# Output products of a SwiGLU feed-forward in three fp32r passes instead of one fp32 product, with the factors made on ScalarE and GpSimd

## The chip, the cores and the metric

The kernel runs on one core of one Trainium2 chip. The metric is the device time of one execution in microseconds (us). Times are medians. PE is TensorE, DVE is VectorE, ACT is ScalarE and POOL is GpSimd.

A ratio of two kernels is the mean time of one kernel's runs over the mean of the other's in the same rounds. So it is not quite the ratio of the medians that are quoted beside it.

## The reference

```python
B, N, m, C = 4, 12416, 32, 128              # x: (B, N, C), inducing: (m, C)
def mab(q, kv):
    s = scale * (q @ kv.transpose(0, 2, 1))
    a = softmax(s)                           # exp after the max is taken off, sum + 1e-9
    return a @ kv
h = mab(I, x); y = mab(x, h)                 # attention over 32 inducing points and back

# y is (B*N, 128) = 49664 tokens; feed-forward with d_ff = 1536, weights given as float64
xn = y / sqrt(mean(y * y) + 1e-6) * rms_g
out = (silu(xn @ w_gate) * (xn @ w_val)) @ w_out
```

## The kernel before

The tokens are cut into 100 units, 25 for each of the four batches: 80 of 512 tokens, 16 of 480 and 4 of 256. A unit goes through 12 blocks of 128 hidden features. One block is a pair of fp32r products (gate, value), a silu on ScalarE, a product on VectorE and one fp32 output product that accumulates over the 12 blocks.

```python
ps_gv = pool("ps_gv", 4, space=PSUM)    # four banks, shared by gate and value products
ps_acc = pool("ps_acc", 2, space=PSUM)
ps_m = pool("ps_m", 2, space=PSUM)      # attention products beside the feed-forward
# ...
for j in range(NJ):                     # NJ = 12 blocks of a unit
    g = ps_gv.tile([P, 512], F32, name="gv", tag="gv")
    nc.tensor.matmul(g[:, 0:T], sg[:, ts(j, P)], a[:, 0:T], start=True, stop=True)   # fp32r
    v = ps_gv.tile([P, 512], F32, name="gv", tag="gv")
    nc.tensor.matmul(v[:, 0:T], sv[:, ts(j, P)], a[:, 0:T], start=True, stop=True)   # fp32r
    sl = silp.tile([P, 512], F32, name="silu")
    nc.scalar.activation(sl[:, 0:T], g[:, 0:T], AF.Silu)
    t = up.tile([P, 512], F32, name="u")
    nc.vector.tensor_tensor(out=t[:, 0:T], in0=sl[:, 0:T], in1=v[:, 0:T], op=ALU.mult)
    for _ in range(slot(j)):            # output products of earlier blocks, 0 to 2 of them
        if late:
            late.pop(0)()
    late.append(lambda j=j, t=t: project(j, t))     # fp32: acc += wo[j]^T t
```

`slot` also places the attention of the next batch and the "seams" among the blocks. A seam is the softmax, the norm and the split of the next 2048 tokens; one comes every four units. Ahead of each big exp of the attention the kernel holds output products back, so that PE has work while ScalarE is busy with the exp and with loading tables. Instructions stay in the order in which the program makes them. Which PSUM bank a new tile gets is decided when the program is built; below, "the built order" is the order of the instructions and of the banks in that program. The "flow" is the feed-forward's main part, from about 100 us on.

## Time and profile before

| | before |
|---|---|
| median of 3 runs | 1749.03 us (1748.61 to 1749.57) |
| PE / ACT / DVE / POOL busy | 99 / 44 / 66 / 10% |
| mean granted PE clock | 0.997 |
| chain of work that ended last | 92% PE |

These are the three lines of the view of PE's waits that the change is going to touch (what waits, for what: us in all, times, longest us):

```profile
PE gv L530 <- ACT silu L534: 2.9, 4, 0.9
...
PE acc L514 <- DVE u L536: 1.6, 1, 1.6
PE gv L532 <- ACT silu L534: 1.4, 7, 0.2
```

L530 is the gate product, L532 the value product, L514 the output product. In 1747 us PE waits for a silu eleven times, 4.3 us in all.

### The profile page before, as it was taken

Reading aid. Unit: us, or ns where it says so; the run is one execution under the profiler, and the core shown is the slowest. Engines: PE = TensorE matmul, PEld = TensorE weight load, DVE = VectorE, ACT = ScalarE, POOL = GpSimd, SP = SyncE. Lnnn points to the kernel's source line nnn. Section 1 sums busy time; section 2 is a strip of 40 time slices with the busy share of each in tenths; the row PEclk is TensorE's granted clock in tenths of the full one; section 3 lists DMA queues with packets and bytes.
Section 4 is the critical chain, followed back from the end, with each engine's and each line's share of the span. In section 5 each row is a group of like instructions: output and inputs, shape, how many; then the busy total and the mean of one; then the engine's idle time right before and its main releaser. Section 6 shows DMA issues by size and latency. Waiting matters only on the chain.

```text
span 1747.0 us, 20705 instructions
## 1 busy us (share of the span) xinstructions
PE 1722.2 (99%) x6454; PEld 973.6 (56%) x6454; DVE 1145.6 (66%) x1985; ACT 765.6 (44%) x1281; POOL 175.6 (10%) x134
## 2 busy tenths in 40 slices
PE   9899999999999999999999999999999999999998
PEld 7545555555565555555556555555556555555555
DVE  4857765666667776666666776566756666656655
ACT  4344445334544445443454444533354444444444
POOL 0311110102101101001010010110201101100100
PEclk9899999999999999999999999999999999999999
DMA  6334462133343145214334316322211121121111
GB/s 243 85 67 79 92 130 54 43 79 66 65 78 62 37 88 119 37 40 99 60 62 81 57 28 130 79 47 63 52 31 33 28 43 30 30 38 36 25 35 23
DMA packets 389340, 112.47 MB, mean 64 GB/s; under 512 B 365136, under 2 KB 369776, under 8 KB 386672
## 3 DMA queue, kind: packets, MB, share of 16 engines
q1 hardware_dynamic: 388944, 111.02, 31.6%
q8 instruction: 51, 0.84, 0.2%
q14 instruction: 57, 0.47, 0.1%
q10 hardware_dynamic: 288, 0.15, 0.0%
HBM read 53.95 MB, written 27.00 MB: 46 GB/s over the span
## 4 chain that ended last, share of the span: by engine, by line
PE 92%; ACT 3%; DVE 2%; DMA 1%; issue 1%; POOL 0%; ACTq 0%; DVEq 0%; POOLq 0%
PE acc L514 55%; PE gv L530 15%; PE gv L532 15%; PE mm L284 2%; PE mm L459 1%; PE mm L341 1%; DMA xn<-in_x_dram 1%; ACT silu L534 1%; PE acc L163 1%; DVE u L536 1%; ACT sc L313 1%; ACT L534 0%; ACT sc L394 0%; PE gv L341 0%; PE mm L407 0%
## 5 line engine op out<-in xcount | busy, mean ns | idle before, releaser
L514 PE MATMUL acc<-u,wo 128*128 128x512 f32 (+2 forms) x2400 | 1199.5, 583 | 3.9 <-POOL wo L241 2.1
L536 DVE TENSOR_TENSOR u<-silu,gv 128x512 f32<-128x512 f32 (+2 forms) x1200 | 798.6, 670 | 559.0 <-ACT silu L534 553.0
L534 ACT ACTIVATE silu<-gv 128x512 f32<-128x512 f32 (+2 forms) x1200 | 699.8, 585 | 931.2 <-DVE u L536 534.8
L530 PE MATMUL gv<-a,sg 128*128 128x512 f32 (+2 forms) x1200 | 919.8, 767 | 5.2 <-ACT silu L534 2.9
L514 PEld LDWEIGHTS acc<-u,wo 128*128 128x128 f32 x2400 | 440.1, 188 | 159.7 <-issue 64.5
L532 PE MATMUL gv<-a,sv 128*128 128x512 f32 (+2 forms) x1200 | 467.2, 389 | 1.9 <-ACT silu L534 1.4
L530 PEld LDWEIGHTS gv<-a,sg 128*128 128x128 f32 x1200 | 227.0, 189 | 279.8 <-issue 261.8
L532 PEld LDWEIGHTS gv<-a,sv 128*128 128x128 f32 x1200 | 227.8, 190 | 276.0 <-issue 186.3
L465 POOL TENSOR_TENSOR z<-z,sc 128x512 f32<-128x512 f32 (+2 forms) x27 | 32.0, 1187 | 1052.3 <-DVE z L464 1012.3
L473 POOL TENSOR_TENSOR rs<-ms,mhalf 128x16 f32<-128x16 f32 (+2 forms) x28 | 75.6, 2700 | 90.8 <-DVE ms L471 90.8
L517 DVE STREAM_TRANSPOSE o<-acc 128x512 f32<-128x512 f32 (+2 forms) x100 | 69.2, 692 | 1.1 <-PE acc L514 0.8
L387 POOL TENSOR_TENSOR sc<-sc,mx 128x512 f32<-128x512 f32 (+2 forms) x24 | 23.2, 968 | 315.8 <-DVE mx L386 244.2
L267 DVE STREAM_TRANSPOSE xT<-xT 128x512 f32<-128x512 f32 (+2 forms) x84 | 53.2, 633 | 0.0
L163 PE MATMUL acc<-ident 128*128 128x128 f32 x220 | 28.0, 287 | 1.4 <-POOL mhalf L150 1.4
L163 PEld LDWEIGHTS acc<-ident 128*128 128x128 f32 x220 | 26.9, 201 | 2.6 <-POOL mhalf L150 1.4
L459 PE MATMUL mm<-eT,gram 128*128 128x512 f32 (+2 forms) x56 | 26.8, 559 | 1.1 <-DVE eT L449 1.1
L284 PE MATMUL mm<-xT,hT 128*32 128x512 f32 (+2 forms) x192 | 26.8, 591 | 0.0
L477 POOL TENSOR_TENSOR sc<-sc,rs 128x512 f32<-128x512 f32 (+2 forms) x27 | 26.4, 976 | 2.1
L341 PE MATMUL mm<-xn,e 128*32 128x128 f32 x582 | 20.7, 276 | 0.0
L284 PE MATMUL mm<-xT,indT 128*32 128x512 f32 (+2 forms) x168 | 20.0, 547 | 0.0
L481 DVE STREAM_TRANSPOSE aT<-sc 128x512 f32<-128x512 f32 (+2 forms) x28 | 18.5, 660 | 1.3 <-POOL sc L477 1.3
L341 PEld LDWEIGHTS mm<-xn,e 128*32 128x32 f32 x582 | 15.0, 109 | 7.7 <-PE gv L530 5.5
(142 smaller groups left out, 432.5 us busy)
## 6 DMA issues: line engine op xcount, KB each, us to landing
out_dram<-o SPq DMA_DIRECT2D x320, 64.0 KB, 2.0
xT<-in_x_dram SPq DMA_DIRECT2D x60, 256.0 KB, 4.6
xn<-in_x_dram SPq DMA_DIRECT2D x60, 256.0 KB, 6.0
a<-hi SPq DMA_DIRECT2D x160, 64.0 KB, 2.0
a<-lo SPq DMA_DIRECT2D x158, 64.0 KB, 2.0
w<-w SPq DMA_DIRECT2D x22, 256.0 KB, 3.4
xn<-in_x_dram SPq DMA_DIRECT2D x5, 1024.0 KB, 11.1
out_dram<-o SPq DMA_DIRECT2D x64, 60.0 KB, 2.0
```

The lines of the kernel that those rows point to most:

```text
L163: nc.tensor.matmul(ps[:, 0:P], ident[:], ident[:], start=True, stop=True)
L267: nc.vector.transpose(out=t[:, ts(k, n * m)], in_=t[:, ts(k, n * m)])
L284: nc.tensor.matmul(ps[ts(q, m), 0:w], lhsT, xT[b, s][:, ts(q, w)], start=True, stop=True)
L341: nc.tensor.matmul(ps[ts(t % R, m), 0:C], e[:, ts(t, m)], xn[:, t, :], start=head and t < R, stop=not more)
L459: nc.tensor.matmul(ps[rows, 0:w], gram[b][rows, rows], st["eT"][rows, 0:w], start=True, stop=True)
L473: nc.gpsimd.tensor_tensor(out=rs, in0=ms, in1=mhalf[rows, 0:n], op=ALU.pow)
L514: nc.tensor.matmul(acc[:, 0:T], wo[:, j, :], t[:, 0:T], start=(j == 0), stop=(j == NJ - 1))
L517: nc.vector.transpose(out=o[:, 0:T], in_=acc[:, 0:T])
L530: nc.tensor.matmul(g[:, 0:T], sg[:, ts(j, P)], a[:, 0:T], start=True, stop=True)
L532: nc.tensor.matmul(v[:, 0:T], sv[:, ts(j, P)], a[:, 0:T], start=True, stop=True)
L534: nc.scalar.activation(sl[:, 0:T], g[:, 0:T], AF.Silu)
L536: nc.vector.tensor_tensor(out=t[:, 0:T], in0=sl[:, 0:T], in1=v[:, 0:T], op=ALU.mult)
```

## The change

The intent is to take work off PE, which is the bound. An fp32 product is four passes through the array, an fp32r product one (the prediction says where the four comes from; in the chain of the kernel before the two take 0.86 and 0.23 us). The change splits weight and input into a high part and a low part and forms the product with three fp32r passes instead of four, by Karatsuba's identity. With w = wh + wl/4096 and u = hi + lo:

w u = (1 + 1/4096) (wh hi + wl lo) + (wl - wh) (hi/4096 - lo)

The first two passes need a PSUM bank of their own. ScalarE takes that bank out at the end of the unit with the factor 1 + 1/4096, and VectorE adds the rest. The bank is taken from the attention, which is left with one. Up to four blocks of a unit are split (j = 0, 3, 6, 9), where a small model of GpSimd's time at build says that the factors will be ready.

```diff
+    KJ = range(0, NJ - 2, 3)
+    SLOT, SPLIT = 1.25, 2.9
-    ps_m = pool("ps_m", 2, space=PSUM)
+    ps_u = pool("ps_u", 1, space=PSUM)
+    ps_m = pool("ps_m", 1, space=PSUM)
 ...
+        def project3(j, hi, lo, d):
+            if st["k"] == nk:
+                st["u"] = ps_u.tile([P, 512], F32, name="u3")
+            ups, i, w = st["u"], KJ.index(j), kws["w"]
+            nc.tensor.matmul(ups[:, 0:T], w[:, i, :], hi, start=st["k"] == nk, stop=False)
+            st["k"] -= 1
+            nc.tensor.matmul(ups[:, 0:T], w[:, NK + i, :], lo, start=False, stop=not st["k"])
+            if not st["k"]:
+                o = st["o"] = outp.tile([P, 512], F32, name="o")
+                nc.scalar.activation(o[:, 0:T], ups[:, 0:T], AF.Copy, scale=1.0 + 2.0 ** -12)
+            project(w[:, 2 * NK + i, :], d)
 ...
         def project(lhsT, rhs):
 ...
+                if nk:
+                    nc.vector.tensor_tensor(out=o[:, 0:T], in0=acc[:, 0:T], in1=o[:, 0:T], op=ALU.add)
-                nc.vector.transpose(out=o[:, 0:T], in_=acc[:, 0:T])
+                nc.vector.transpose(out=o[:, 0:T], in_=(o if nk else acc)[:, 0:T])
 ...
+        def three(j, t):
+            nc.scalar.activation(hi, v, AF.Copy, scale=1.0 - 2.0 ** -13)
+            nc.gpsimd.tensor_tensor(out=lo, in0=v, in1=hi.bitcast(F32), op=ALU.subtract)
+            def rest():                 # one slot later
+                nc.scalar.activation(hs[:, 0:T], hi.bitcast(F32), AF.Copy, scale=2.0 ** -12)
+                nc.gpsimd.tensor_tensor(out=d, in0=hs[:, 0:T], in1=lo.bitcast(F32), op=ALU.subtract)
+                kara.append((ready[b, u, j], lambda: project3(j, hi, lo, d)))
 ...
-                if hold and len(late) < LAG or len(late) < 2:
-                    return 0
-                return 2 if len(late) > 2 else 1
+                count = max(len(plain) - 1, 0) + sum(at <= now for at, _ in kara)
+                if hold and count < LAG - 1:
+                    return
+                for _ in range(min(count, 2)):
+                    if kara and kara[0][0] <= now:
+                        kara.pop(0)[1]()
+                    else:
+                        plain.pop(0)()
```

Left out are the splitting of the weights, the build-time model, and the steps of the attention, which are moved by a few slots.

More of the change, by code (lines that the diff above doesn't have):

```diff
@@ L89 @@
     NU = len(units)
+    KJ = range(0, NJ - 2, 3)
+    NK = len(KJ)
+    SLOT, SPLIT = 1.25, 2.9
     def pool(name, bufs, **kw):
@@ L103 @@
     halves = pool("halves", 1)
-    astk = pool("astk", 3)
+    astk = pool("astk", 2)
+    third = pool("third", 1)
     silp = pool("silp", 3)
-    up = pool("up", LAG + 2)
+    up = pool("up", LAG + 3)
     outp = pool("outp", 2)
@@ L121, in load_rows @@
         n = per[s]
-        t = xnat[b, s] = xnp.tile([P, n, C], F32, name=f"xn{s}")
+        t = xnat[b, s] = xnp.tile([P, 16 if b and n > 4 else n, C], F32, name=f"xn{s % 2 if b and n > 4 else s}")
         if b or s == full:
             for q in range(R):
-                nc.sync.dma_start(out=t[ts(q, m), :, :], in_=of(xrows, b, s)[q])
+                nc.sync.dma_start(out=t[ts(q, m), 0:n, :], in_=of(xrows, b, s)[q])
         else:
@@ L247 @@
     flowing = []
+    lent = []
     def attention(b, load_next):
@@ L258, in bank @@
             if flowing:
+                assert not lent
                 return ps_m.tile([P, 512], F32, name="mm", tag="mm")
@@ L361, in turn_h, with scale_h, square_h @@
             nc.vector.tensor_copy(out=hT[:], in_=ps[:, 0:P])
-        def square_h():
+            if b:
+                scale_h()
+        def scale_h():
             hg = st["hg"] = once.tile([P, P], F32, name="hg")
             nc.vector.tensor_scalar_mul(out=hg[:], in0=st["ps"][:, 0:P], scalar1=gam[:])
+        def square_h():
+            if not b:
+                scale_h()
             gram[b] = small.tile([P, P], F32, name="gram")
@@ L457, in square @@
         def square():
+            assert not lent
+            lent.append(s)
             ps = st["ps"] = ps_m.tile([P, 512], F32, name="mm", tag="mm")
@@ L462, in turn_z @@
             ps = st["ps"]
+            lent.clear()
             z = st["z"] = work.tile([P, n, m], F32, name="z", tag="work")
@@ L496, in gather, with split_wo @@
             queue.dma_start(out=a[ts(k, m), 0:w].bitcast(F32), in_=half[ts(q, m), 0:w].bitcast(F32))
-    late, waiting = [], []
+    plain, kara, waiting = [], [], []
+    kws = {}
     def soon(k, step):
         waiting.append([k, step])
+    def split_wo():
+        w = kws["w"] = xnp.tile([P, 3 * NK, C], F32R, name=f"xn{full - 1}")
+        whi, wlo, ws = (w[:, ts(k, NK), :] for k in range(3))
+        wk = wo[:, KJ.start:KJ.stop:KJ.step, :]
+        nc.vector.tensor_scalar_mul(out=whi, in0=wk, scalar1=1.0 - 2.0 ** -13)
+        nc.vector.tensor_tensor(out=wlo, in0=wk, in1=whi.bitcast(F32), op=ALU.subtract)
+        nc.vector.tensor_scalar_mul(out=wlo, in0=wlo.bitcast(F32), scalar1=4096.0)
+        nc.vector.tensor_tensor(out=ws, in0=wlo.bitcast(F32), in1=whi.bitcast(F32), op=ALU.subtract)
+        for k, name in enumerate(("hi", "lo", "d")):
+            kws[name] = xnp.tile([P, 4, 512], F32R, name=f"xn{full - 4 + k}")
     def ffn(b, u, slot):
@@ L511, in ffn, with project @@
         acc = ps_acc.tile([P, 512], F32, name="acc")
-        def project(j, t):
-            nc.tensor.matmul(acc[:, 0:T], wo[:, j, :], t[:, 0:T], start=(j == 0), stop=(j == NJ - 1))
-            if j + 1 == NJ:
-                o = outp.tile([P, 512], F32, name="o")
-                nc.vector.transpose(out=o[:, 0:T], in_=acc[:, 0:T])
-                soon(2, lambda: store(o))
+        nk = sum((b, u, j) in ready for j in range(NJ))
+        st = {"left": NJ, "k": nk}
+        if nk:
+            st["o"] = None
+        def project(lhsT, rhs):
+            nc.tensor.matmul(acc[:, 0:T], lhsT, rhs, start=st["left"] == NJ, stop=st["left"] == 1)
+            st["left"] -= 1
+            if not st["left"]:
+                o = st["o"] if nk else outp.tile([P, 512], F32, name="o")
+                if nk:
+                    nc.vector.tensor_tensor(out=o[:, 0:T], in0=acc[:, 0:T], in1=o[:, 0:T], op=ALU.add)
+                nc.vector.transpose(out=o[:, 0:T], in_=(o if nk else acc)[:, 0:T])
+                soon(2, lambda: store(o))
+        def project3(j, hi, lo, d):
[9 more added lines that the diff above has]
+            project(w[:, 2 * NK + i, :], d)
         def store(o):
@@ L526, in store @@
                 nc.sync.dma_start(out=d[:, :, ts(k, m)], in_=o[ts(k, m), 0:T].rearrange("p (t c) -> p t c", c=m))
+        def three(j, t):
+            n = kws["n"] = (kws.get("n", 0) + 1) % 4
+            hi, lo, d = (kws[name][:, n, 0:T] for name in ("hi", "lo", "d"))
+            v = t[:, 0:T]
+            nc.scalar.activation(hi, v, AF.Copy, scale=1.0 - 2.0 ** -13)
+            nc.gpsimd.tensor_tensor(out=lo, in0=v, in1=hi.bitcast(F32), op=ALU.subtract)
+            def rest():
+                hs = third.tile([P, 512], F32, name="hs")
+                nc.scalar.activation(hs[:, 0:T], hi.bitcast(F32), AF.Copy, scale=2.0 ** -12)
+                nc.gpsimd.tensor_tensor(out=d, in0=hs[:, 0:T], in1=lo.bitcast(F32), op=ALU.subtract)
+                kara.append((ready[b, u, j], lambda: project3(j, hi, lo, d)))
+            soon(1, rest)
         for j in range(NJ):
@@ L536, in ffn @@
             nc.vector.tensor_tensor(out=t[:, 0:T], in0=sl[:, 0:T], in1=v[:, 0:T], op=ALU.mult)
-            for _ in range(slot(j)):
-                if late:
-                    late.pop(0)()
-            late.append(lambda j=j, t=t: project(j, t))
+            slot(j)
+            if (b, u, j) in ready:
+                soon(1, lambda j=j, t=t: three(j, t))
+            else:
+                plain.append(lambda j=j, t=t: project(wo[:, j, :], t[:, 0:T]))
     f = attention(0, B > 1)
@@ L633, in schedule @@
     def schedule(b):
-        plan, marks = {}, []
+        plan, marks, busy = {}, [], {}
         def add(k, step, *args):
             plan.setdefault(int(k), []).append(lambda: step(*args))
+            if getattr(step, "__name__", "") == "sub_max" and args[0]:
+                busy[int(k)] = 1.1
         if not b:
@@ L649, in schedule @@
                 add(k, step, *args)
+            add(18, split_wo)
             for s in range(1, NS):
@@ L664, in schedule @@
                 add(at + 14, g["scores1"], s)
-                add(97 + 6 * s, load_rows, b + 1, s)
-                add(140 + 6 * s, g["turn_e"], s)
-                add(144 + 6 * s, g["sum_h"], s)
-                add(194 + 8 * s, g["scores2"], s)
-                add(198 + 8 * s, g["sub_max"], s)
-            for k, name in ((126, "max1"), (128, "max2"), (130, "max3"), (134, "exp1"), (184, "end_h"), (186, "turn_h"),
-                            (188, "square_h")):
+                add(97 + 6 * s if s < 2 else 130 + 7 * s, load_rows, b + 1, s)
+                add(140 + 7 * s, g["turn_e"], s)
+                add(143 + 7 * s, g["sum_h"], s)
+                add(199 + 7 * s, g["scores2"], s)
+                add(203 + 7 * s, g["sub_max"], s)
+            for k, name in ((126, "max1"), (128, "max2"), (130, "max3"), (134, "exp1"), (189, "end_h"), (191, "turn_h"),
+                            (193, "square_h")):
                 add(k, g[name])
@@ L674, in schedule @@
                 add(175 + 18 * i, g["fetch"], i)
-                add(191 + 12 * i, g["stack"], i)
+                add(195 + 13 * i, g["stack"], i)
                 for k in range(R):
-                    add(193 + 12 * i + k, g["place"], i, k)
+                    add(197 + 13 * i + k, g["place"], i, k)
             add(254, g["exp2"], 0, NS)
@@ L682, in schedule @@
                 add(k, load_channels, *pieces[b + 2].pop(0))
-        return plan, marks
-    seams = {}
+        return plan, marks, busy
+    seams, seam_busy = {}, {}
     order = [(b, s) for b in range(B) for s in range(NS)]
@@ L698 @@
                 n, j = divmod(j, NJ)
-                seams.setdefault((b, firsts[s] + n + late_by, j), []).append(step)
+                at = (b, firsts[s] + n + late_by, j)
+                seams.setdefault(at, []).append(step)
+                seam_busy[at] = seam_busy.get(at, 0) + {3: 1.4, 4: 3.0, 5: 1.2}.get(i, 0)
     flat = [(b, u) for b in range(B) for u in range(NU)]
     after = dict(zip(flat, flat[1:]))
+    plans = [schedule(b) for b in range(B)]
+    free, ready = 0.0, {}
+    for b, u in flat:
+        plan, marks, busy = plans[b]
+        for j in range(NJ):
+            k = u * NJ + j
+            now = (b * NU * NJ + k) * SLOT
+            free = max(free, now) + busy.get(k, 0) + seam_busy.get((b, u, j), 0)
+            begin = max(free, now + 2.2 * SLOT)
+            if (j not in KJ or b == 0 and u < 2 or (b, u) == flat[-1] or begin > now + 3.2 * SLOT or
+                    any(k - 2 <= e <= k + 6 for e in marks)):
+                continue
+            free = begin + SPLIT
+            ready[b, u, j] = int((free + 0.3) / SLOT) + 1
     for b in range(B):
-        plan, marks = schedule(b)
+        plan, marks, _ = plans[b]
         held = () if b else range(2, 10)
@@ L710, in slot @@
                 k = u * NJ + j
+                now = b * NU * NJ + k
                 for one in waiting:
                     one[0] -= 1
-                while waiting and not waiting[0][0]:
-                    waiting.pop(0)[1]()
+                for one in [one for one in waiting if not one[0]]:
+                    waiting.remove(one)
+                    one[1]()
                 for step in plan.get(k, ()):
@@ L720, in slot @@
                     gather(*after[b, u])
+                count = max(len(plain) - 1, 0) + sum(at <= now for at, _ in kara)
                 hold = k in held or any(k < e <= k + LAG - 2 for e in marks)
-                if hold and len(late) < LAG or len(late) < 2:
-                    return 0
-                return 2 if len(late) > 2 else 1
+                if hold and count < LAG - 1:
[3 more added lines that the diff above has]
+                        kara.pop(0)[1]()
+                    else:
+                        plain.pop(0)()
             ffn(b, u, slot)
-    while late:
-        late.pop(0)()
+    while kara or plain:
+        (plain.pop(0) if plain else kara.pop(0)[1])()
     for _, step in waiting:
```

## The prediction

> **What bounds the kernel now.** I first read the page's busy times, then its chain of work that ended last, then the groups by line, then one quiet stretch of the chain, and last the only kind of place where TensorE (PE) waits for its own consumers.
>
> ```profile
> PE 1722.2 (99%) x6454; PEld 973.6 (56%) x6454; DVE 1145.6 (66%) x1985; ACT 765.6 (44%) x1281; POOL 175.6 (10%) x134
> ...
> PE 92%; ACT 3%; DVE 2%; DMA 1%; issue 1%; POOL 0%; ACTq 0%; DVEq 0%; POOLq 0%
> ...
> L536 DVE TENSOR_TENSOR u<-silu,gv 128x512 f32<-128x512 f32 (+2 forms) x1200 | 798.6, 670 | 559.0 <-ACT silu L534 553.0
> L534 ACT ACTIVATE silu<-gv 128x512 f32<-128x512 f32 (+2 forms) x1200 | 699.8, 585 | 931.2 <-DVE u L536 534.8
> ```
>
> TensorE is busy for 99% and makes 92% of the chain: the end moves with PE's work plus any new PE stall. The other three compute engines have room on average.
>
> The chain in a quiet stretch (start, us, what) gives the real cost of the pieces, which the group means (767, 389 and 583 ns, ends modelled) do not:
>
> ```profile
> 804.52 0.23 PE gv L530
> 804.75 0.23 PE gv L532
> 804.99 0.86 PE acc L514 x2
> 805.85 0.23 PE gv L530
> ```
>
> One block is two fp32r products of 0.23 us and one fp32 product of 0.86 us. Successive silus start 1.32 us apart (1514.12, 1515.44, 1516.76), so 0.465 for the pair and 0.855 for the fp32 product. An fp32 pass is then 0.214 us, an fp32r pass 0.2325.
>
> When no fp32 product stands between pairs, four PSUM buffers (two pairs) are too few. The kernel holds products back ahead of an exp, and there the chain shows:
>
> ```profile
> 270.00 0.61 ACT silu L534
> 270.61 0.04 issue
> 270.65 0.50 PE gv L532
> 271.15 0.24 PE gv L530
> ```
>
> The value product waits for a silu to free its buffer, and having waited takes 0.50 us instead of 0.23. From that run's first gate product, which by the usual 0.27 us before its silu starts at 269.73, eight products took until 272.57, or 2.84 us, where eight of 0.2325 are 1.86. The 0.98 are two such stalls: 0.49 us each, about 0.22 waited and 0.27 of restart. The kernel before has only some six such bursts in the flow, two for each exp of a batch but the last, so PE loses about 10 us to waits altogether.
>
> **What the Trainium skill says.** "FP8 and Floating Point Precision", section TensorE Precision Notes, gives true FP32 as four passes; the trace agrees, 0.855 against 0.2325. "TensorE: Matmul & The Clock Gate", section Back-to-back issue gap, gives N/2.4 + 2.5 ns, 216 ns at 512 columns: the fp32 pass measures 214, the fp32r pass 232, about 17 more than the page, and I use the measured one. "ScalarE: Activation LUTs", section What ACT_TABLE_LOAD costs, says that back-to-back activations overlap by some 93 ns. The trace agrees: two silus of 0.60 us, ready together, occupy 1.09 us. I therefore space ready ScalarE instructions 0.50 us apart (0.52 where the source is SBUF; an SBUF activation of 512 took 615 to 630 ns).
>
> **The change part by part.**
>
> *Removed from PE.* By the order of the built program 337 of the 1200 output products become three fp32r passes: 277 of 512 columns, 48 of 480, 12 of 256. A 512 one saves 0.855 - 3 x 0.2325 = 0.158 us. At 480 columns a block takes 1.24 us with starts 0.22 apart for fp32r, so 0.80 - 0.66 = 0.14. At 256 I estimate 0.05. Sum: 43.7 + 6.7 + 0.6 = 51 us, or 2.9%. That is the ceiling.
>
> *Added beside it.* ScalarE: two copies for each of 325 large blocks (0.6 us) and one evacuation for each of 94 large units, 744 x 0.6 = 446 us, to some 70% of the span. GpSimd: 650 two-input operations; the like z product took 1.28 us, so 830 us, to some 58%. VectorE: 94 adds of 0.69 us, 65 us, to some 69%. No engine becomes the bound by its sum. The new factors come in time: from the gate product of block j, the first copy starts at 2.09 us, GpSimd's low factor ends near 4.1, the second copy at 3.7, the last factor near 5.4; the program places the three passes at 6.1. GpSimd needs 2.6 us in a 3.8 us round of three blocks.
>
> *Moved on PE.* The new order of a round of three blocks is: pair 0, one fp32 product, pair 1, pair 2 at once, then the three passes and an fp32 product: 3.81 us where it was 3.96. So 324 pairs now follow a pair with nothing between, against about two dozen before. If the value product of pair 2 waits on VectorE's product of pair 0, there is slack: silu from 0.27 to 0.87, product to 1.59, needed at 2.02. But buffers are given out in the order of release at build time, and in 86 of the 324 the value product gets the bank of the gate product just ahead of it, almost always (67 times) three slots after the unit's end. It then waits for a silu that ends 0.87 us after its gate product, plus 0.05, while PE reaches it after 0.70: the burst measured above, 0.49 us each. 86 x 0.49 = 42 us.
>
> *The unit's end.* ScalarE runs silu 1, copy, silu 2, copy, evacuation: started at 1.59 with 0.50 to 0.52 spacing, the evacuation ends at 4.23. VectorE's add then ends at 4.96, the transpose, which depends on it, at 5.70, and the next product at 6.31, against a PE that wants its bank at 5.83. Mostly (above) the wait was moved onto a silu by the bank order, and the bank is wanted only after the passes, at about 8. In eight units it was not: five at 0.48 + 0.27 and three, where the add waits for a later product, at about 1.3: 8 us.
>
> *Small things.* Splitting the weights is 2.2 us of VectorE once (four operations of 0.43 to 0.69 us, as its like ones on 512 columns took), with about 1 us of slack; the single attention bank and VectorE's late work at the seams, some 5 us together, an estimate from slacks of about 0 to 0.5 us at 24 seams.
>
> *Sum:* 1749 - 51 + 42 + 8 + 5 = 1753 us. I shade this to 1746, because some of the 86 waits may fall where PE had already been delayed and cost less than a full stall.
>
> **The rivals.**
> - *PE's saving arrives whole.* For it: other engines stay under 75%, and in the kernel before PE waits almost never. Against it: the bursts of pairs, which already stall where they occur. Time: 1749 - 51 + 5 = about 1703.
> - *The unit's end becomes the wait.* If the bank order does not protect PE, each of 94 units loses 0.75 us or, with the seam's extra VectorE work (23 units, 1.2 us more), near 2: 70 + 28 us of stalls added to the 42, less 51, about 1840. The bank order in the built program speaks against it.
> - *GpSimd is late.* Its two operations wait behind a 2.9 us power and 1.3 us products at the seams. The placing leaves out blocks there and gives 2.9 us for a split, so I expect no more than a few waits. If each of the 24 seams had one of 1 to 2 us, 1780.
> - *GpSimd and VectorE in each other's way.* "SBUF — State Buffer", section SBUF: two separate sides, has them share a port pair for VectorE operations with two SBUF inputs or in a two-port mode. The new add and the main product read PSUM on one side, so only the 24 seams' splits collide: within the 5 us. No run here shows a collision yet.
>
> **Range and chances.** The saving of 51 us is the firm term; the 42 us is a count from the order times one measured stall, and could be anything from 15 (the waits mostly absorbed) to 60 (each delays the next round too). So 1746 us, with 8 in 10 between 1708 and 1785. Faster by over 2% means below 1714, which needs stalls under 16 us: 0.16. Slower by over 2% means above 1784, which needs the second rival in part: 0.10. Within 2%: 0.74.
>
> **What would show it.** In the profile after, the chain should show the passes at 0.23 us each and a round of 3.81 us when quiet. PE's waits should list the value product on silu some 70 to 90 times at about 0.2 us by the profile (each costing 0.49 in the chain), and on VectorE's product only in a handful. PE's busy share should fall a little, and ScalarE, VectorE and GpSimd stand near 70, 69 and 58%. I am wrong if waits of PE on GpSimd's factors reach tens of us, if the passes take over 0.25 us, or if value products wait on VectorE's product in most units.

## The result, and the profile after

| | before | after |
|---|---|---|
| median | 1748.82 us (1748.55 to 1749.57, 4 runs) | 1774.47 us (1771.11 to 1777.91, 4 runs) |
| ratio | | 1.0146, 95% interval 1.0125 to 1.0167 |
| mean granted PE clock | 0.997 | 0.992 |

The time is within 2% of before, which is what the prediction held likeliest, and inside its range. But it is 28 us above the predicted 1746 us, and the change costs time rather than saving it. The page of the kernel after answers the lines of before: busy times, the chain by engine, and the groups of VectorE's product (L608) and the silu (L606).

```profile
PE 1710.4 (96%) x6791; PEld 1030.0 (58%) x6791; DVE 1213.1 (68%) x2086; ACT 1122.5 (63%) x2052; POOL 1026.0 (58%) x808
...
PE 87%; ACT 6%; DVE 2%; issue 2%; DMA 1%; POOL 1%; SPq 0%; ACTq 0%; DVEq 0%; POOLq 0%
...
L608 DVE TENSOR_TENSOR u<-silu,gv 128x512 f32<-128x512 f32 (+2 forms) x1200 | 788.9, 665 | 495.4 <-ACT silu L606 386.8
L606 ACT ACTIVATE silu<-gv 128x512 f32<-128x512 f32 (+2 forms) x1200 | 696.2, 581 | 530.5 <-PE gv L602 383.4
```

No engine has become the bound by its sum: POOL went from 10 to 58%, ACT from 44 to 63%. What changed is the chain, where PE's part fell from 92 to 87% and ScalarE's doubled to 6%. PE now waits for ScalarE. The view of PE's waits says where:

```profile
PE gv L604 <- ACT silu L606: 18.3, 82, 0.2
PE gv L602 <- ACT silu L606: 9.9, 7, 1.8
PE mm L483 <- DVE wlo L433: 4.3, 3, 1.4
PE mm L483 <- DVE sc L304: 4.0, 2, 2.2
PE gv L604 <- DVE u L608: 3.6, 8, 0.8
PE acc L555 <- POOL xn L595: 3.2, 4, 2.5
```

The value product (L604) waits for a silu 82 times where it waited 7 times, always 0.2 us at most. The waits of the other five rows are few, and most are longer. L602 is the gate product behind an exp; L483 is an attention product that waits for its single bank; the last row is a pass that waits for a factor of GpSimd.

A quiet stretch of the chain shows that the passes themselves cost what they should (start, us, what; L568, L570 and the first of the "x3" are the three passes):

```profile
1433.59 0.23 PE gv L602
...
1435.38 0.23 PE gv L602
1435.61 0.23 PE gv L604
1435.84 0.23 PE u L568
1436.07 0.23 PE u L570
1436.30 1.09 PE acc L555 x3
1437.39 0.23 PE gv L602
```

From one gate product to the same place in the next round it is 1437.39 - 1433.59 = 3.80 us. The round before was three times 1.32 us, or 3.96. So each quiet round saves 0.16 us. Some 9 us later in the chain, shortly after a unit's end, comes what takes it away:

```profile
1446.31 0.25 PE gv L602
...
1446.58 0.61 ACT silu L606
...
1447.23 0.50 PE gv L604
```

Two pairs stand back to back here. The chain runs from the gate product of the first (1446.31) through its silu to the value product of the second (1447.23), which was given the bank that this silu has to free. The value product starts 0.92 us after that gate product, where three products of 0.23 us would have had it start at 0.70, and then takes 0.50 us instead of 0.23. The 0.22 waited and the 0.27 of slower start (the "restart") make 0.49 us: one such place eats what three quiet rounds save. Taken over all 81 such waits of the flow, from the end of one product to the end of the next, the trace gives the same 0.49 us.

One more thing was not in the prediction. The next view has windows of the kernel after (window, its length, busy us and count of PE, PEld, DVE, ACT, POOL, then the granted PE clock, DMA share and GB/s), around two of the long waits:

```profile
175.00:180.00 5.00, 2.76 (x14) 0.91 (x13) 4.80 (x11) 2.23 (x4) 1.45 (x2) 1.00 0.16 24
180.00:185.00 5.00, 5.00 (x12) 2.79 (x11) 1.08 (x3) 0.60 (x1) 1.51 (x2) 0.66 0.70 109
1324.00:1332.00 8.00, 8.00 (x16) 4.14 (x17) 3.07 (x7) 2.78 (x6) 1.26 (x2) 0.57 0.00 0
```

The clock is full while PE waits and low afterwards, while PE is busy all the time. The trace's record of the granted clock has it at exactly half from 180.6 us for 3.41 us and from 1324.0 us for 6.83 us. There are four such stretches between 100 us and the end of the flow, 17.1 us together. The kernel before has none there.

### The profile page after: what moved, and what is told of

Its sections match the earlier page's. It is cut to its first block, busy times and chain, and to the rows that moved or that the text cites. A ratio compares the mean times of both kernels' runs of the same rounds, so it can differ in the third digit from the quotient of the medians.

```text
span 1773.4 us, 23241 instructions
## 1 busy us (share of the span) xinstructions
PE 1710.4 (96%) x6791; PEld 1030.0 (58%) x6791; DVE 1213.1 (68%) x2086; ACT 1122.5 (63%) x2052; POOL 1026.0 (58%) x808
## 4 chain that ended last, share of the span: by engine, by line
PE 87%; ACT 6%; DVE 2%; issue 2%; DMA 1%; POOL 1%; SPq 0%; ACTq 0%; DVEq 0%; POOLq 0%
PE acc L555 43%; PE gv L604 15%; PE gv L602 14%; PE u L568 4%; PE u L570 4%; ACT silu L606 4%; PE mm L300 2%; PE mm L483 1%; PE mm L357 1%; DVE u L608 1%; DMA xn<-in_x_dram 1%; PE acc L177 1%; ACT L606 0%; PE gv L357 0%; POOL rs L498 0%
## 5 line engine op out<-in xcount | busy, mean ns | idle before, releaser
L608 DVE TENSOR_TENSOR u<-silu,gv 128x512 f32<-128x512 f32 (+2 forms) x1200 | 788.9, 665 | 495.4 <-ACT silu L606 386.8
L606 ACT ACTIVATE silu<-gv 128x512 f32<-128x512 f32 (+2 forms) x1200 | 696.2, 581 | 530.5 <-PE gv L602 383.4
L555 PE MATMUL acc<-u,wo 128*128 128x512 f32 (+2 forms) x1726 | 865.9, 585 | 2.6 <-POOL wo L255 2.0
L602 PE MATMUL gv<-a,sg 128*128 128x512 f32 (+2 forms) x1200 | 798.5, 666 | 11.8 <-ACT silu L606 9.9
L590 POOL TENSOR_TENSOR xn<-u,xn 128x512 fp32r<-128x512 f32 (+2 forms) x337 | 430.1, 1276 | 494.0 <-ACT xn L589 312.3
L604 PE MATMUL gv<-a,sv 128*128 128x512 f32 (+2 forms) x1200 | 480.2, 400 | 22.2 <-ACT silu L606 18.3
L595 POOL TENSOR_TENSOR xn<-hs,xn 128x512 fp32r<-128x512 f32 (+2 forms) x337 | 422.4, 1253 | 28.0 <-POOL xn L590 2.8
L604 PEld LDWEIGHTS gv<-a,sv 128*128 128x128 f32 x1200 | 227.9, 190 | 276.3 <-issue 133.3
L555 PEld LDWEIGHTS acc<-u,wo 128*128 128x128 f32 x1726 | 320.6, 190 | 97.7 <-issue 26.6
L602 PEld LDWEIGHTS gv<-a,sg 128*128 128x128 f32 x1200 | 228.0, 190 | 243.7 <-issue 130.8
L589 ACT ACTIVATE xn<-u 128x512 fp32r<-128x512 f32 (+2 forms) x337 | 207.5, 616 | 64.1 <-DVE u L608 63.7
L594 ACT ACTIVATE hs<-xn 128x512 f32<-128x512 f32 (+2 forms) x337 | 207.6, 616 | 0.0
L568 PE MATMUL u<-xn,xn 128*128 128x512 f32 (+2 forms) x337 | 142.1, 422 | 0.0
L555 PE MATMUL acc<-xn,xn 128*128 128x512 f32 (+2 forms) x337 | 132.0, 392 | 3.2 <-POOL xn L595 3.2
L570 PE MATMUL u<-xn,xn 128*128 128x512 f32 (+2 forms) x337 | 130.5, 387 | 0.0
L568 PEld LDWEIGHTS u<-xn,xn 128*128 128x128 f32 x337 | 63.5, 188 | 22.4 <-issue 15.9
L570 PEld LDWEIGHTS u<-xn,xn 128*128 128x128 f32 x337 | 63.5, 188 | 16.8 <-issue 4.7
L561 DVE STREAM_TRANSPOSE o<-o 128x512 f32<-128x512 f32 (+2 forms) x97 | 67.7, 698 | 3.3
```

What stands on the lines that cost most here:

```text
L555: nc.tensor.matmul(acc[:, 0:T], lhsT, rhs, start=st["left"] == NJ, stop=st["left"] == 1)
L568: nc.tensor.matmul(ups[:, 0:T], w[:, i, :], hi, start=st["k"] == nk, stop=False)
L570: nc.tensor.matmul(ups[:, 0:T], w[:, NK + i, :], lo, start=False, stop=not st["k"])
L589: nc.scalar.activation(hi, v, AF.Copy, scale=1.0 - 2.0 ** -13)
L590: nc.gpsimd.tensor_tensor(out=lo, in0=v, in1=hi.bitcast(F32), op=ALU.subtract)
L594: nc.scalar.activation(hs[:, 0:T], hi.bitcast(F32), AF.Copy, scale=2.0 ** -12)
```

## The experiments

All ran three rounds, with the kernel before in the same rounds (median 1749.4 to 1749.8 us).

### e1_spread: one output product per slot unless more than two are due

```diff
-                for _ in range(min(count, 2)):
+                for _ in range(min(count, 2 if count > 2 else 1)):
```

The same work and the same split, but 41 pairs directly follow a pair in the built order instead of 324.

> Same blocks split, but at most one product per slot unless three are waiting, so that a product nearly always stands between two pairs: 41 pairs follow a pair at once by the built order instead of 324, and 23 instead of 86 of these take the bank of the gate product just ahead. Theory (back-to-back pairs waiting 0.49 us for the silu just started are the largest loss): waits of the value product on silu fall from 82 to 25 or fewer, and the time by some 60 x 0.49 = 30 us, to about 1744. Rival (the load on ScalarE, GpSimd and the single attention bank cost the time, whatever the order on PE): 1768 to 1778.

Measured: 1729.53 us (1728.41 to 1731.42), ratio 0.9886 (0.9872 to 0.9901). The waits of the value product fell from 82 to 21, and those of the gate product stayed:

```profile
PE gv L602 <- ACT silu L606: 11.7, 7, 1.9
PE gv L604 <- ACT silu L606: 4.7, 21, 0.2
```

What follows: the tight order of the pairs cost 45 us, nearly as much as the split saves. One line gives them back and makes the kernel faster than both. The gain is more than the theory allowed, and more than 61 waits of 0.49 us (30 us) explain. The eight waits of the value product on VectorE's product are gone as well (3.6 us, 5.8 with restarts); the remaining 9 us were not assigned.

### e2_fixed_banks: two banks for the gate product, two for the value product

```diff
-    ps_gv = pool("ps_gv", 4, space=PSUM)
+    ps_gv = pool("ps_gv", 2, space=PSUM)
+    ps_v = pool("ps_v", 2, space=PSUM)
-            v = ps_gv.tile([P, 512], F32, name="gv", tag="gv")
+            v = ps_v.tile([P, 512], F32, name="v", tag="v")
```

The instruction order stays that of the change. The value product can no longer get the bank of a gate product, so it waits for VectorE's product of two blocks before.

> Order of the changed kernel kept, but gate and value products get two PSUM banks each, so a value product always waits for VectorE's product of two pairs before and never for a silu just started. Theory (the banks given out in release order shield PE from the unit's end, where VectorE's product comes late behind evacuation, add and transpose): waits on silu vanish, waits on VectorE's product appear in most units, 0.76 us each instead of 0.49 and 1.2 us more at some 20 seams: 1800 to 1812. Rival (the bank order itself is the fault, the unit's end is harmless): the 82 waits vanish with nothing in their place, 1730 to 1738.

Measured: 1841.71 us (1841.57 to 1843.42), ratio 1.0529 (1.0513 to 1.0544).

```profile
PE v L605 <- DVE u L609: 80.4, 100, 2.6
```

The waits on the silu are gone, and one at each unit's end has come in their place, 0.80 us on average and up to 2.6. The direction was expected; the size was 30 us above the range. At the seams a wait is about 2 us or more, and in thirteen stretches between 100 us and the end of the flow the clock is halved. What follows: the four shared banks, though they cause the 82 waits, protect PE from something worse. The prediction's second rival is this case, and its 98 us of stalls at the unit's end were about right (80.4 us, 107 with restarts). That its total of 1840 us was met is luck: it also held the 42 us of stalls on the silu, which e2 does not have, and did not hold the thirteen stretches (44 us at half speed, worth some 22).

### e3_no_split: the moved order alone, no block split

```diff
-            if (j not in KJ or b == 0 and u < 2 or (b, u) == flat[-1] or begin > now + 3.2 * SLOT or
+            if (True or j not in KJ or b == 0 and u < 2 or (b, u) == flat[-1] or begin > now + 3.2 * SLOT or
```

> Everything of the changed kernel but the split: no block takes three passes; the moved attention steps, the one attention bank, the pools stay. Theory (these moves cost a part of the 24 us of loss that is not the 82 waits, some 10): 1755 to 1762. Rival (the moves and the single bank are the main loss): 1770 or more. Second rival (they cost nothing): 1747 to 1752.

Measured: 1751.65 us (1750.88 to 1752.29), ratio 1.0011 (0.9994 to 1.0028). The theory expected too much; the second rival is right. The moved attention steps, the single attention bank and the buffers cost some 2 us when nothing is split, and at most 5 by the interval. The long waits of the attention product for its single bank (8.3 us after the change) are absent here. They come only with the split; but making the factors on ScalarE and GpSimd is not needed for them, since e6, which makes none, still has 5.9 us of them in the same five places.

### e4_three_blocks: three blocks of a unit instead of four

```diff
-    KJ = range(0, NJ - 2, 3)
+    KJ = range(0, NJ - 3, 3)
```

The block nearest to the unit's end is left in fp32: 273 products are split instead of 337, which takes some 10 us of saving away.

> Three of twelve blocks at most instead of four: 273 split instead of 337. Theory (the loss comes once per unit, the gain with each block): 64 x 0.156 = 10 us of saving lost, the waits on silu as many or a few more (97 by the built order): 1783 to 1790. Rival (each split block brings its own loss): faster than the changed kernel, 1765 to 1771.

Measured: 1792.60 us (1791.56 to 1793.24), ratio 1.0245 (1.023 to 1.0261). The waits of the value product for the silu did not go down with the splits but are 88 of 19.5 us, and those for the single bank rose from 8.3 to 12.6 us. The theory holds in direction and is 3 us short; the rival falls. What follows: the stalls are not in proportion to the number of split products, so fewer splits only lose the gain.

### e5_one_bank: all three passes into the accumulator, no evacuation and no add

```diff
-            nc.tensor.matmul(ups[:, 0:T], w[:, i, :], hi, start=st["k"] == nk, stop=False)
-            nc.tensor.matmul(ups[:, 0:T], w[:, NK + i, :], lo, start=False, stop=not st["k"])
-            (evacuation by ScalarE, add by VectorE)
+            project(w[:, i, :], hi)
+            project(w[:, NK + i, :], lo)
             project(w[:, 2 * NK + i, :], d)
```

The factor 1 + 1/4096 is left out, which makes the split products less exact. PE's order stays, with the same 324 adjacent pairs. ScalarE and VectorE have nothing new at the unit's end.

> The changed kernel's order on PE, but all three passes accumulate in the unit's own bank: no evacuation by ScalarE, no add by VectorE (the factor 1 + 2^-12 is left out, so the result is wrong on purpose by about 1e-4 of a quarter of the sum; it may still pass). Theory (the unit's end, evacuation then add then transpose ahead of VectorE's next product, is what makes a pair right behind a pair stall): 324 pairs still follow a pair at once, but only 34 take the bank of the gate product ahead; PE's waits on silu fall from 82 to about 35, time to 1738 to 1752. Rival (pairs back to back cost by themselves): as many waits, 1765 or more.

Measured: 1742.93 us (1740.03 to 1744.46), ratio 0.9957 (0.994 to 0.9974), as the theory expected.

```profile
PE gv L599 <- ACT silu L601: 6.7, 30, 0.2
```

30 waits instead of 82. In the built order, 34 of the 324 adjacent value products get the bank of the gate product just ahead, where the change has 86. What follows: it is the evacuation and the add at the end of a unit that shift the order in which banks come free at build. PE meets the shift three slots later as a wait on a silu. 52 fewer waits of 0.49 us are 25 of the 31 us that e5 gains on the change, though the engines of the two instructions have room. Two stretches at half clock fewer (6.8 us in e5, 17.1 in the change) are worth some 5 more.

### e6_given_factors: e1 with constant factors

```diff
-            nc.scalar.activation(hi, v, AF.Copy, scale=1.0 - 2.0 ** -13)
-            nc.gpsimd.tensor_tensor(out=lo, in0=v, in1=hi.bitcast(F32), op=ALU.subtract)
-                hs = third.tile([P, 512], F32, name="hs")
-                nc.scalar.activation(hs[:, 0:T], hi.bitcast(F32), AF.Copy, scale=2.0 ** -12)
-                nc.gpsimd.tensor_tensor(out=d, in0=hs[:, 0:T], in1=lo.bitcast(F32), op=ALU.subtract)
```

The tiles of the factors are filled once from the weights. The output is wrong (relative error 0.53). PE does the same passes, and nothing is made for them.

> Order of e1_spread on PE, but the three moving factors are constant tiles: no copies on ScalarE and no subtractions on GpSimd (wrong result on purpose). e1_spread loses 32 us against the before time less the saving. Theory (a good part of these 32 comes from the load of the splits: waits on GpSimd's factors, ScalarE's copies around the exps and the seams): 1705 to 1715. Rival (the rest is PE's order, the hold before an exp and the unit's end): 1722 to 1730.

Measured: 1725.10 us (1722.14 to 1725.98), ratio 0.9856 (0.9839 to 0.9872). The rival is right: making the factors costs e1 only 4 us, on 1348 instructions of ScalarE and GpSimd. What e1 still loses lies in PE's order, the exps and the seams.

### e7_spread_seam: e1 with the steps of the seam moved

```diff
-                j = ((14, 14, 17, 18, 21, 21, 33) if k else (32, 32, 33, 33, 34, 34, 37))[i]
+                j = ((14, 14, 18, 19, 22, 22, 33) if k else (32, 32, 33, 33, 34, 34, 37))[i]
-                    any(k - 2 <= e <= k + 6 for e in marks)):
+                    any(k - 2 <= e <= k + 9 for e in marks)):
```

Squaring, turning, scaling and applying come one slot later, and no block within nine slots ahead of an exp is split.

> e1_spread with two small moves: the seam's square product and what follows it one slot later, so that it does not meet the single attention bank still unread, and no split within nine slots ahead of an exp instead of six (331 split instead of 337: 1 us of saving lost). Theory (PE's waits of 7 us on the attention bank and 12 us on silu at the exps[...] are what e1_spread still loses): 1715 to 1723. Rival (those waits only move elsewhere): 1727 to 1732.

Measured: 1773.75 us (1771.67 to 1774.60), ratio 1.0136 (1.0121 to 1.0151). This was a miss of 50 us.

```profile
PE acc L555 <- POOL xn L595: 23.3, 23, 2.1
```

The pass now waits for the low factor of GpSimd at 23 places, 1.0 us each; there are 24 seams. GpSimd's power at the seam (2.7 us on average in the changed kernel) and a product of 1.05 us now come between the two subtractions of one block, just ahead of its last factor. With restarts these waits are 29.5 us (23.3 + 23 x 0.27). Nine stretches at half clock (34 us, against 14 in e1) are worth some 10 and the exps 5 more, which is about the 44 us to e1; but smaller rows moved too, in both directions, and the sum was not closed. What follows: the prediction's third rival, GpSimd late at every seam, is real and lies one slot away. In the change it appears in only 4 waits because the seam's steps stand where they stand.

### e8_five_blocks: e7 with five blocks of a unit

```diff
-    KJ = range(0, NJ - 2, 3)
+    KJ = range(0, NJ - 2, 2)
```

> e7_spread_seam with every second block offered for the split, five of twelve at most; 351 are split by the built order, as GpSimd's planned time allows no more. Theory (GpSimd has room: 2.6 us in some 3.4): 20 x 0.157 = 3 us better than e7_spread_seam, but 154 pairs follow a pair again, 12 of them onto the bank just ahead: within 4 us of it. Rival (GpSimd is late when splits stand closer): 1735 or more, with PE's waits on GpSimd over 10 us.

Measured: 1805.96 us (1801.52 to 1811.50), ratio 1.0324 (1.03 to 1.0348), with 351 products split.

```profile
PE gv L604 <- DVE u L608: 30.6, 34, 1.7
```

It is slower, as the rival said, but the waits are on VectorE's product, the long ones at a unit's end. Behind them stands GpSimd after all, as the prediction's fourth rival has it (GpSimd and VectorE in each other's way). VectorE's scaling of 16 columns at the seam, first in the kernel before and then here:

```profile
L454 DVE TENSOR_SCALAR l<-l 128x16 f32<-128x16 f32 x20 | 3.5, 175 | 0.7
...
L476 DVE TENSOR_SCALAR l<-l 128x16 f32<-128x16 f32 x20 | 18.2, 908 | 0.7
```

It took 0.18 us and takes 0.91 on average, up to 1.30. In the five microseconds before 25 of the 34 waits (29.0 of the 30.6 us) the trace has this scaling, or the cast or subtraction of the split, stretched in this way, always beside a subtraction of GpSimd. Since e8 was built on e7, it says nothing on five blocks in e1's order. In the build, 154 pairs are adjacent again.

### e9_spread_square: e1 with only the squaring and the turn one slot later

```diff
-                j = ((14, 14, 17, 18, 21, 21, 33) if k else (32, 32, 33, 33, 34, 34, 37))[i]
+                j = ((14, 14, 18, 19, 21, 21, 33) if k else (32, 32, 33, 33, 34, 34, 37))[i]
```

> The order of the first experiment (one product per slot unless more than two are due), with the squaring of the output and the step after it one slot later at the seams. In the first experiment the attention products on the single bank wait for the VectorE scale ahead of them and for the split of the weight, in the changed kernel 7.3 us over five rows, and one such wait of 2.2 us is followed by a stretch at half clock. If those waits are the rest of what the order costs: 1720 to 1727 us. If the steps only move the waits to other slots: 1728 to 1732 us, as the first experiment. If GpSimd becomes late, as in the seventh experiment, where more of the steps were moved: above 1740 us, with waits for xn on the accumulating products.

Measured: 1726.65 us (1725.16 to 1727.07), ratio 0.9866 (0.985 to 0.9882). It was run at another time.

The two rows of the attention product for its single bank, 7.0 us in e1 (8.3 in the changed kernel, not the 7.3 of the expectation), are down to 1.2 us, and GpSimd is not late. The time is 3 us below e1; the runs of the two do not overlap, but the intervals of their ratios do. So the waits were worth less than their 7 us, and how much is not settled.

### e10_spread_fixed: e1 with the fixed banks of e2

> The order of the first experiment (41 pairs that directly follow a pair instead of 324) with two banks fixed for the gate product and its passes and two for the value product, where the change takes any of four in turn. Theory: the order of the banks matters only where pairs follow each other directly, and the second experiment's waits of the value product for VectorE's product at the end of a unit came from such pairs: 1727 to 1737 us. Rival: the fixed banks themselves tie the value product to VectorE's product of two pairs before, which the end of a unit makes late whatever the order: 1770 us or more, with waits of the value product for u of about 2 us at most of the unit ends.

The edit is that of e2 on top of that of e1. Measured: 1774.42 us (1771.26 to 1775.27), ratio 1.0136 (1.0119 to 1.0153). The theory falls and the rival's time is met: 51 waits, though of 0.5 us on average and not of about 2. Nine stretches at half clock (41 us, against 14 in e1) come with them.

```profile
PE v L605 <- DVE u L609: 26.0, 51, 2.1
```

The chain at one unit's end shows what the value product waits for (start, us, what):

```profile
1418.73 0.69 DVE o L561
...
1419.44 0.03 DVE o L562
...
1420.08 0.66 DVE u L609
...
1420.78 0.50 PE v L605
```

L561 is the add that the change brought, L562 the transpose behind it; the next product on VectorE comes after both. With fixed banks the value product needs that product's bank, and is late although no pairs are adjacent to speak of. With shared banks e1 is 45 us faster. In e1's built program, 170 of the 300 value products in blocks 5 to 7, where VectorE is late, get the bank of the gate product one block before, and mostly an output product lies between, so that its silu is done in time. What follows: sharing the banks is an advantage when something stands between the pairs, and becomes the cost when nothing does.

### e11_longer_hold: e9 with more products held back ahead of an exp

```diff
-                hold = k in held or any(k < e <= k + LAG - 2 for e in marks)
-                if hold and count < LAG - 1:
+                hold = k in held or any(k < e <= k + LAG - 1 for e in marks)
+                if hold and count < LAG:
-                for _ in range(min(count, 2 if count > 2 else 1)):
+                for _ in range(min(count, 2 if count > 2 or any(e <= k < e + 5 for e in marks) else 1)):
```

> The ninth experiment with products held back over one slot more ahead of an exp (up to five instead of four) and issued two per slot for five slots from the exp on. In the ninth experiment the gate product still waits for silu 12.0 us in eight places behind an exp, the longest 1.9 us, where the kernel before waits 2.9 us in four. Theory: they wait there because too few products were held back; one or two products more (0.86 us each) cover most of it, so these waits fall under 5 us and the time to 1716 to 1722 us. Rival: in the longer hold the pairs have nothing between them and wait for banks (0.49 us each), and a wait that is no longer than the one it replaces is only moved: 1724 to 1730 us.

Measured: 1719.86 us (1718.29 to 1720.82), ratio 0.983 (0.9814 to 0.9846), as the theory expected.

```profile
PE gv L604 <- ACT silu L606: 5.3, 24, 0.2
...
PE gv L602 <- ACT silu L606: 3.4, 5, 1.0
```

The gate product's waits behind an exp fell from 12.0 us (e9) to 3.4, and after the first 150 us no stretch at half clock is left in the flow. This kernel beats the kernel before by 1.7% and, by the medians, the changed one by 3.1% (1719.86 / 1774.47 = 0.969), at the same work. It ran on another chip than e1 to e10, but the kernel before took the same time there (1749.39 us), and the two ratios give the same 0.969. It is the best.

## Why the prediction was right or wrong

"Within 2%" and its range were right, and so was the main reason, the stalls on the silu; the number was 28 us too low. By its steps:

- **The removed passes: right.** The fp32r passes take 0.23 us in the chain, and the quiet round is 3.80 us where 3.81 was predicted (the prediction's own terms add up to 3.80). All 337 splits are there: PE's instructions rose by 337, from 6454 to 6791, three in place of the two of an fp32 product for each split. The 216 ns that the prediction quotes are what the page gives for an isolated product; for a stream the same section measures about 131 ns at 512 columns, and no stream of these kernels comes near that (0.214 and 0.2325 us a pass).
- **Other engines no bound: right.** ScalarE, VectorE and GpSimd stand at 63, 68 and 58%, where 70, 69 and 58% were predicted. ScalarE grew by 357 us where 446 were added up; the prediction summed whole durations, and back-to-back activations, which overlap, count once in the busy time (all of ScalarE's durations after the change add up to 1240 us, and 1122 are busy).
- **The stalls of the value product on the silu: right.** 86 were counted in the built order, 82 show in the waits, at 18.3/82 = 0.22 us, as predicted, each 0.49 us with the restart. The chain shows one. e1 and e5, which take most of them away by two different means, both come out faster than the change, by 45 and 31 us.
- **The unit's end in eight places: right by luck.** There are 8 waits on VectorE's product, 3.6 us, with the restarts (8 x 0.27) 5.8 us where 8 was predicted. But only two of them (0.18 us each) come within 2 us after a unit's add; before the others no add lies within 11 us. The three longest (0.80 us each) follow a subtraction of the attention (L409) that took 1.42 us on VectorE, where it took 0.69 in the kernel before.
- **GpSimd and VectorE in each other's way: it happens, and is small here.** Those three subtractions began while a subtraction of GpSimd ran. The same is seen at the split of the seam, first before and then after the change:

```profile
L484 DVE TENSOR_TENSOR lo<-aT,hi 128x480 fp32r<-128x480 f32 x4 | 2.6, 658 | 0.1
...
L509 DVE TENSOR_TENSOR lo<-aT,hi 128x480 fp32r<-128x480 f32 x4 | 5.6, 1402 | 0.1
```

In turn, 16 of GpSimd's subtractions that began beside a split took up to 1.77 us instead of 1.28. Without GpSimd's subtractions (e6) the same split is back at 0.66 us, and in e1, with them, at 1.39. So the sharing that the prediction quotes from the skill is seen here, and not only at the splits: e8 shows a cast and a scaling stretched too. VectorE's main product is not touched (686 and 681 ns on average at 512 columns). In the changed kernel all this lengthens VectorE's work by some 14 us and GpSimd's by 9 (34 and 19 instructions, against their usual durations in the kernel before), of which the three waits above (2.4 us, 3.2 with restarts) reach PE; smaller delays were not looked for.
- **The other rivals.** The saving did not arrive whole: the bursts of pairs, which the prediction named against it, took most of it. The second rival came about only with the banks fixed (e2), the third only with the seam moved (e7). Their totals (1840 and 1780 us, measured 1841.7 and 1773.8) were met by luck in part: both held the 42 us of stalls on the silu, which are gone in e2 and nearly so in e7 (5 waits), and neither held the half clock.
- **"The single attention bank and VectorE's late work at the seams, some 5 us together": this term was mis-sized, and three costs were missing from the sum.** The bank alone cost 9.7 us. GpSimd's late factors ("no more than a few waits": there were four) had been given no time, and longer waits behind the exps and a lower clock had not been thought of. Each against the kernel before:

| what | waited | with restarts of 0.27 us |
|---|---|---|
| attention product for its single bank | 8.3 us, 5 times | 9.7 us |
| gate product behind an exp | 9.9 us, 7 times (before 2.9, 4 times) | 7.8 us more |
| pass for GpSimd's factor | 3.2 us, 4 times | 4.3 us |
| another attention product (L429; the view does not say for what it waits) | 1.9 us, 3 times | 2.7 us |
| half clock after long waits | 17.1 us at half speed | 8.5 us |
| sum | | 33 us |

- **The shading from 1753 to 1746: wrong.** It assumed that some stalls would be absorbed. None were to speak of.

With measured terms the sum is 1749 - 51 + 37 (75 more waits on a silu than before) + 5 (the eight waits on VectorE's product, less 0.4 waited before) + 33 = 1773 us. Measured were 1774.5.

The waits behind the exps were there to be asked about: the page of the kernel before lists them (2.9 us), and the prediction looked at these places only for their bursts of pairs. e11 shows that holding more back repairs this part; why the same hold covered less after the change was not settled. The half clock could not be seen in the kernel before, whose one longer wait in the flow (1.6 us) nothing followed. That long waits bring it on is an inference from the order in time: in e3 the longest wait in the flow is 1.7 us and there is no stretch at half clock; in e11 there is one wait of 2.4 us, and the one stretch begins in its last half microsecond. Against a simple rule stands e1, where a wait of 2.2 us (at 141 us) is followed by no stretch. No run tests it alone. The 8.5 us are half of 17.1; the products of PE in these stretches, each against its usual spacing, give about the same (8.4 us).

## What to carry to other kernels

When work is taken off the bounding engine, what stood between two instructions goes with it: look at which buffer the next instruction gets, and from whom, in the built order, since a shared pool that hides a late engine when the order is loose exposes the nearest one when it is tight. Spreading the issue evenly (one line) was worth 45 us here, nearly the whole arithmetic saving of 51. Add the restart to each short wait (0.22 us waited cost 0.49), and reckon that a wait near 2 us on TensorE may cost more than its length. When GpSimd gets work, look for VectorE instructions that grew longer (0.18 to 0.91 us in e8), since the view of the waits then names VectorE and not GpSimd. And check where the predicted waits fall, not only how many there are.

## What the Trainium skill lacked or had wrong

- "TensorE: Matmul & The Clock Gate", section HAM oscillation — how this bites in real kernels, puts the rule as no PE-idle gaps over about 3.4 us. Here shorter waits were followed by half clock: 2.46, 2.24, 1.79 and 1.79 us in the changed kernel, with stretches of 3.41 or 6.83 us. A third wait of 1.79 us and seven of 1.43 to 1.75 us in it were not followed by one, and in e1 one of 2.17 us was not, so there is no sharp limit in the length alone. The length of a stretch agrees with the window that the page describes; that a gap has to fill the window does not.
- No page gives, as such, the cost of a restart of a stream of 512-column fp32r products after a short wait; it would have to be put together from what the page on TensorE gives for one product and for a weight load. Here the value product took 0.50 us instead of 0.23, so 0.22 us of waiting cost 0.49.
- "GPSIMD Engine Reference", section 3.1 Elementwise — side-by-side cycle accounting, gives about 2.6 cycles an element for a two-input operation, which at its 1.2 GHz would be 1.11 us for 512 columns (an estimate from the page). The factors of this kernel took 1.28 us each at 512 columns and 0.73 at 256. The 0.55 us between them for 256 columns are the page's rate; what the page lacks is a measured fixed cost of an instruction, some 0.17 us here.
